# Two-layer linear attention and MLP on one core: dummies from a ready constant, some behind the first transposes, and the key weights in one load

## The chip, the core and the metric

The kernel runs on one core of one Trainium2 chip. The metric is the device time of one execution in microseconds (us), as the median of three runs; lower is better. All times inside an execution are counted from the start of the span that the profiler recorded. The engines are TensorE (PE, with its weight loads as PEld), VectorE (DVE), ScalarE (ACT), GpSimd (POOL) and SyncE (SP, which only issues DMAs here).

## The reference, cut to what matters

The input is one sequence of 2048 tokens with 512 features in bf16. Two blocks alternate, each twice, with the same weights:

```python
phi = lambda t: jnp.where(t > 0, t + 1, jnp.exp(t)) + 1e-6
# A: linear attention, 32 heads of 16
q, k, v = split(layernorm(x) @ wqkv)
pq, pk = phi(q), phi(k)
kv = einsum("bhsd,bhse->bhde", pk, v);  z = einsum("bhsd->bhd", pk)
o = einsum("bhqd,bhde->bhqe", pq, kv) / (einsum("bhqd,bhd->bhq", pq, z)[..., None] + 1e-6)
x = x + o @ wo
# B: MLP of width 1792
x = x + gelu(layernorm(x) @ w1 + b1) @ w2 + b2
```

The attention sums over all 2048 tokens, so nothing behind it can start before every key tile has been seen.

## The kernel before, in words

The tokens form 16 tiles of 128 rows, four tiles to a chunk. Layer 0 takes the chunks in the order `C0=(3, 0, 1, 2)`, so the first tiles are 12, 13, 14, 15, and then 0 to 11. Everything stays in SBUF.

`build_kernel` only describes the work as a graph of named operations, each with an engine, an estimated duration and what it reads and writes. A `Scheduler` (line 111) then takes the order of the operations on each engine from hand-stored lists, `CONF["ORDER"]` (line 325), one list for each of the five engines; its clock (a cost for each operation, and for DMAs a modelled bus, lines 178 to 183) serves to choose buffers and PSUM banks, and `assign_waits` (line 265) puts in the semaphore waits. On the chip each engine works through its list strictly in order, so an instruction that waits holds up all behind it on its engine. `CONF["WAY"]` says which engine does an operation that could go to several, and whether a transpose goes through PE (`pe`) or through a DMA (`dma`).

The names carry the layer and the tile. For tile 12 of layer 0:

- `x0`, `x1`, `x2` load tiles 12, 13, and 14 with 15 (lines 642 to 646); `xc0`, `xc1`, `xc2` load the other chunks (line 638); `wk0` and `wk1` are the two halves of the key weights, 256 KB each, on SP and on ACT (line 648); `wq` is the query weights, 512 KB (line 651). All but `wk1` are on SP.
- `statsA0_12`, `aggrA0_12`, `vepsA0_12`, `powA0_12` make the mean and 1/std (lines 720 to 735). In the first chunk the tile is only centred first (`cenA0_12`, line 701), the 1/std is applied later as the scale of the activations, and `yscA0_12` (lines 739 to 747) scales the centred tile itself for the G products. Tile 13 gets its sums from ACT instead (`sumA0_13`, `sqA0_13`, lines 708 and 715). Tiles 0 to 11 are normed at once by `normA0_...`, on DVE (line 760) or ACT (line 755).
- `PTA0_12` is four PE transposes of 128 by 128 (line 783) and `tcA0_12` the ACT copy out of PSUM (line 793); tiles transposed by DMA have `TA0_...` on SP instead (line 770).
- `K0_12` is the key product (four matmuls of 512 columns, line 838), `Q0_3_0` the query product of tile 12 (line 856, chunk 3; lines 869 for chunks that are not done by token). Each is followed by `exp...` and `relu...` on ACT (lines 808 and 819) and `min...`, `phi...` on DVE or POOL (lines 821 and 825, or 812 and 814).
- `G0_12_0` collects the product of keys and normed tokens (line 939). `Z0_c` sums a chunk's keys (line 920), `zs0_c` adds them up on DVE (line 929), `zb0` builds the block matrix for the denominators (line 1000), and `D0_...` are the denominators (line 1063) with `ln...` and `rec...` on ACT (lines 1065 and 1067). `KV0`, `M0` (lines 994 and 1017), `WO0` (line 1087) finish the attention; `PTB0_0`, `W10` (line 1119) and `W20` (line 1157) are the MLP. Layer 1 has the same names with 1.

In PSUM the key and query tiles of the first chunk, their transposes and the dummies share the four banks 4 to 7; banks 0 to 3 hold the running G.

PE begins with `warm` (line 678): seven dummy matmuls of 512 columns and one of 128 on `onesm`, a tile that DVE fills first (`ones`, line 641). Weights of the later stages (`wv`, `wo`, `w1_0`, `w1_1`, `w2_0`, `w2_1`, function `late`, line 664) are loaded from POOL's queue behind all transposes of layer 0. `b2` (line 1193) is the load of the last bias, copied to 128 partitions, and stands on SP between two transposes; `b1` and `Tb1` (lines 1191 and 1214) load and transpose the other bias and `b1c` on ACT (line 1215) copies it.

The lists before, up to where they matter for the change:

```python
"pe":  "warm PTA0_12 PTA0_13 K0_12 K0_13 PTA0_14 Q0_3_0 Q0_3_2 PTA0_15 K0_14 G0_12_0 Q0_3_1 K0_15 G0_13_0 "
       "G0_14_0 Q0_3_3 PTA0_1 K0_0 K0_1 G0_15_0 K0_3 ..."
"act": "wk1 sumA0_13 tcA0_12 tcA0_13 sqA0_13 reluk0_12 expk0_12 tcA0_14 expk0_13 reluk0_13 ..."
"sp":  "x0 x1 wk0 x2 wq xc0 xc1 xc2 TA0_0 TA0_3 TA0_2 TA0_8 TA0_4 b2 TA0_6 TA0_7 ..."
```

Of the kernel before, what the change touches and what calls it, by code (L numbers as in the profile page):

```python
# [6 lines left out]
BF16 = mybir.dt.bfloat16  # L7
# [3 lines left out]
P = 128  # L11
S = 2048
D = 512
# [97 lines left out]
class Scheduler:  # L111
# [12 lines left out]
    def run(self):  # L124
# [14 lines left out]
        for _ in g.ops:  # L139
# [38 lines left out]
            if e == "sp" or o.sem is not None:  # L178
                if o.name[0] == "T":
                    o.end = max(at + o.lat, bus + 1000.0 if bus > at + 300.0 else 0.0)  # L180
                else:
                    bus = max(at + (1300.0 if at < 1400.0 else 1700.0 if e == "pool" else 900.0), bus) + o.nbytes
                    o.end = bus + o.lat
            else:
                o.end = at + dur + o.lat
# [79 lines left out]
def assign_waits(graph, order, sems, dma_sems):  # L265
# [10 lines left out]
    while len(done) < total:  # L276
        moved = False
        for e in ENGINES:
# [43 lines left out]
    C0=(3, 0, 1, 2), N_WARM=7, ZC=(0, 3), LQ='sp', N_HALF=1, N_K=4, N_Q=3, P_Z0=6.15, N_PB=1, N_PT=8, P_DEN=-50.43,  # L322
# [4 lines left out]
            "warm PTA0_12 PTA0_13 K0_12 K0_13 PTA0_14 Q0_3_0 Q0_3_2 PTA0_15 K0_14 G0_12_0 Q0_3_1 K0_15 G0_13_0 "  # L327
            "G0_14_0 Q0_3_3 PTA0_1 K0_0 K0_1 G0_15_0 K0_3 G0_0_0 K0_2 Q0_0_2 Q0_0_0 G0_1_0 K0_8 Z0_3 K0_4 G0_2_0 "
            "K0_6 G0_3_0 Q0_0_3 K0_7 K0_5 G0_4_0 K0_10 K0_11 Z0_0 K0_9 Q0_1_2 Q0_1_3 Z0_1 Q0_0_1 Q0_1_0 Z0_2 "
            "G0_5_0 G0_6_0 D0_0_3 D0_0_0 G0_7_0 Q0_1_1 D0_0_1 G0_8_0 D0_0_2 G0_9_0 G0_10_0 G0_11_0 G0_11_2 G0_11_1 "  # L330
            "D0_1_0 Q0_2_0 G0_11_3 KV0_0 KV0_1 D0_1_1 ZR0 KV0_2 KV0_3 Q0_2_1 D0_1_2 M0_0 M0_1 M0_2 M0_3 Q0_2_2 "
            "WO0_0_0 WO0_0_1 WO0_0_2 WO0_0_3 D0_1_3 WO0_1_0 WO0_2_0 WO0_3_0 Q0_2_3 WO0_4_0 WO0_7_0 WO0_6_0 PTB0_0 "
            "WO0_5_0 W10_0_5_0 W10_0_1_0 W10_0_9_0 W10_0_6_0 W10_0_2_0 W10_0_3_0 W10_0_12_0 W10_0_7_0 W10_0_0_0 "
            "W10_0_4_0 W10_0_13_0 W10_0_11_0 W10_0_8_0 W10_0_10_0 W20_0_0 W20_1_0 W20_0_7 W20_1_7 W10_0_9_1 "
            "W10_0_1_1 W10_0_7_1 W10_0_8_1 W10_0_5_1 W10_0_6_1 W10_0_12_1 W10_0_0_1 W10_0_13_1 W10_0_3_1 "
            "W10_0_11_1 W10_1_4_0 W10_1_13_0 W10_0_4_1 W10_1_11_0 W10_1_0_0 W10_1_3_0 W10_1_2_0 W10_0_2_1 "
            "W10_1_6_0 WO0_9_0 WO0_8_0 WO0_11_0 W10_1_5_0 W10_1_8_0 W10_1_10_0 WO0_10_0 W10_0_10_1 W10_1_1_0 "
            "W10_1_12_0 W10_1_7_0 W10_1_9_0 W20_7_0 W20_4_0 W20_7_7 W20_4_7 WO0_15_0 W20_5_0 W20_2_0 W20_5_7 "
# [189 lines left out]
def build_kernel(nc, A_x, A_wqkv, A_wo, B_x, B_w1, B_b1, B_w2, B_b2, out, conf=None, report=False):  # L528
# [5 lines left out]
    with ExitStack() as es:  # L534
# [48 lines left out]
        def bank(t, n=512):  # L583
            return ps[:, t.slot, 0:n]
# [767 lines left out]
```

## Time and profile before

| what | value |
|---|---|
| median of three runs (lowest to highest) | 328.75 us (328.06 to 329.84) |
| the profiled execution, its own time | 330.35 us |
| its span, first to last instruction | 328.6 us |
| PE busy | 322.0 us of the span |
| first dummy, first key matmul | 1.51 us, 6.52 us |
| first W1 matmul of layer 0 | 65.61 us |
| end of the last matmul group | 326.0 us |

The span is 1.75 us shorter than the execution's own time, and the profiled execution is 1.6 us longer than the median. In a timeline row the first number is the start, the second how long the merged group lasted, then engine, line, operation, what is written from what, and in brackets how long the engine stood idle before and what released it. A matmul's recorded duration contains its drain (379 ns is common for one of 512 columns), so the rate of a stream is read from the starts of its groups, not from their durations. The row PEclk of the page shows the throttle's grant, and is at full speed in all 40 slices.

### The profile page before, as it was taken

How to read it: one execution, taken by the hardware profiler on the slowest of the kernel's cores; microseconds unless marked ns; L12 is line 12 of the kernel's file. 1: busy time of each engine (PE TensorE's matmuls, PEld its weight loads, DVE VectorE, ACT ScalarE, POOL GpSimd, SP SyncE). 2: the span in 40 equal slices, each digit the busy share in tenths (PEclk: the TensorE clock that was granted, in tenths of full speed). 3: DMA queues.
4: the chain of work that ended last, by engine and by line, in shares of the span. 5: the costliest groups of instructions: out<-in, count | busy, mean ns of one | idle time of the engine just before them, and what ended most of it. 6: DMA issues, size and time to landing. Idle time of an engine off the chain costs nothing.

```text
span 328.6 us, 4769 instructions
## 1 busy us (share of the span) xinstructions
PE 322.0 (98%) x1716; PEld 159.1 (48%) x1716; DVE 223.0 (68%) x507; ACT 194.4 (59%) x334; POOL 133.1 (41%) x223
## 2 busy tenths in 40 slices
PE   7999999999999999999999999999999999999996
PEld 2444545476544444444444444448644444444444
DVE  4799599999794554575158899999989776100132
ACT  4898769783747055536984377878933452567200
POOL 3366646567447105533047725756903176000000
PEclk9999999999999999999999999999999999999999
DMA  6324593105404300312101110022044214200011
GB/s 231 152 49 98 121 358 149 18 16 97 49 0 66 80 16 3 64 32 48 34 16 32 35 32 0 2 49 50 18 96 99 48 33 97 64 0 2 16 48 64
DMA packets 47027, 20.37 MB, mean 62 GB/s; under 512 B 41948, under 2 KB 45532, under 8 KB 47004
## 3 DMA queue, kind: packets, MB, share of 16 engines
q1 hardware_dynamic: 45676, 15.09, 20.7%
q0 software_dynamic: 1056, 4.72, 4.1%
q8 instruction: 13, 0.21, 0.3%
q10 hardware_dynamic: 272, 0.26, 0.3%
q14 instruction: 10, 0.08, 0.1%
HBM read 8.00 MB, written 2.10 MB: 31 GB/s over the span
## 4 chain that ended last, share of the span: by engine, by line
PE 94%; DMA 2%; DVE 1%; ACT 1%; issue 0%; SPq 0%; ACTq 0%
PE ps L1119 30%; PE ps L1157 29%; PE ps L838 9%; PE ps L1087 8%; PE ps L856 5%; PE ps L971 4%; PE ps L939 3%; PE ps L869 2%; DMA wqkv<-in_A_wqkv_dram 1%; DMA t<-yb 1%; PE ps L1144 1%; PE ps L1063 1%; PE ps L1017 1%; PE ps L994 1%; PE ps L783 0%
## 5 line engine op out<-in xcount | busy, mean ns | idle before, releaser
L1125 ACT ACTIVATE gT<-ps,b1c 128x512 bf16<-128x512 f32 (+1 forms) x140 | 77.0, 601 | 53.8 <-PE ps L1119 53.3
L1119 PE MATMUL ps<-t,w 128*128 128x512 bf16 (+1 forms) x560 | 101.3, 336 | 0.4 <-issue 0.4
L1157 PE MATMUL ps<-w,gT 128*128 128x512 bf16 x434 | 97.3, 379 | 0.0
L1119 PEld LDWEIGHTS ps<-t,w 128*128 128x128 bf16 x560 | 54.6, 98 | 43.6 <-ACT t L793 1.2
L1157 PEld LDWEIGHTS ps<-w,gT 128*128 128x128 bf16 x434 | 42.5, 98 | 50.8
L808 ACT ACTIVATE eb<-ps 128x512 bf16<-128x512 f32 x56 | 32.5, 602 | 31.0 <-PE ps L838 25.6
L735 POOL TENSOR_TENSOR rstd<-veps,neghalf 128x1 f32<-128x1 f32 x64 | 37.8, 598 | 8.3 <-DVE veps L733 5.9
L1167 DVE TENSOR_TENSOR outb<-ps,xsb 128x512 bf16<-128x512 f32 x15 | 10.2, 683 | 40.2 <-PE ps L1157 38.7
L838 PE MATMUL ps<-wqkv,t 128*128 128x512 bf16 x128 | 33.6, 394 | 1.4 <-DMA t<-yb 0.7
L720 DVE BATCH_NORM_STATS2 stats<-xsb 128x6 f32<-128x512 f32 x48 | 32.0, 680 | 0.3
L1087 PE MATMUL ps<-gtb,t 128*128 128x512 bf16 x128 | 30.9, 379 | 0.0
L760 DVE TENSOR_SCALAR yb<-xsb,mv,rstd 128x512 bf16<-128x512 f32 x28 | 16.7, 602 | 13.6 <-POOL rstd L735 13.4
L733 POOL TENSOR_SCALAR veps<-mv 128x1 f32<-128x1 f32 x28 | 7.4, 276 | 43.7 <-DVE mv L722 43.0
L755 ACT ACTIVATE yb<-xsb,nmr,rstd 128x512 bf16<-128x512 f32 x20 | 15.7, 811 | 14.6 <-POOL nmr L752 14.6
L819 ACT ACTIVATE rb<-ps 128x512 bf16<-128x512 f32 x38 | 21.8, 601 | 0.2 <-PE ps L838 0.2
L821 DVE TENSOR_SCALAR eb<-eb 128x512 bf16<-128x512 bf16 x46 | 14.4, 325 | 10.1 <-ACT eb L808 10.0
L725 POOL TENSOR_SCALAR veps<-mv 128x1 f32<-128x1 f32 x32 | 8.8, 274 | 29.1 <-DVE mv L722 27.2
L838 PEld LDWEIGHTS ps<-wqkv,t 128*128 128x128 bf16 x128 | 12.3, 100 | 17.0 <-issue 1.7
L856 PE MATMUL ps<-wqkv,t 128*128 128x512 bf16 x80 | 20.3, 383 | 0.0
L1163 DVE TENSOR_TENSOR xsb<-ps,xsb 128x512 f32<-128x512 f32 x16 | 11.0, 688 | 13.2 <-PE ps L1157 13.1
L1087 PEld LDWEIGHTS ps<-gtb,t 128*128 128x128 bf16 x128 | 12.3, 98 | 15.1 <-DVE mv L722 0.5
L1104 POOL TENSOR_TENSOR xsb<-xsb,b2b 128x512 f32<-128x512 f32 x14 | 17.4, 1255 | 2.8 <-ACT yb L755 1.6
(103 smaller groups left out, 395.2 us busy)
## 6 DMA issues: line engine op xcount, KB each, us to landing
w<-in_B_w_dram POOLq DMA_DIRECT2D x4, 896.0 KB, 9.8
out_dram<-outb SPq DMA_DIRECT2D x15, 128.0 KB, 2.0
t<-in_A_x_dram SPq DMA_DIRECT2D x3, 512.0 KB, 7.3
t<-yb SPq DMA_TRANSPOSE x56, 2.5
wqkv<-in_A_wqkv_dram SPq DMA_DIRECT2D x1, 512.0 KB, 5.8
wo<-in_A_wo_dram POOLq DMA_DIRECT2D x1, 512.0 KB, 4.6
wqkv<-in_A_wqkv_dram POOLq DMA_DIRECT2D x1, 512.0 KB, 7.4
t<-t SPq DMA_TRANSPOSE x20, 2.5
```

The costliest lines, as they stand in the source:

```text
L720: G.op("dve", lambda e: e.bn_stats(stats[:, s.slot, :], src()), 620, reads=src_keys, writes=[k + "s"], tiles=[s, *src_tiles], prio=prio, n ...
L735: G.op("pool", lambda e: e.tensor_tensor(rstd[:, s.slot:s.slot + 1], veps[:, s.slot:s.slot + 1], neghalf[:], op=ALU.pow), 570, reads=[k + ...
L760: G.op("dve", lambda e: e.tensor_scalar(yb[:, y.slot, :], src(), stats[:, s.slot, 2:3] if by_act else mv[:, s.slot, 0:1], rstd[:, s.slot:s ...
L808: G.op("act", lambda e: e.activation(eb[:, et.slot, :], bank(bt), ACT.Exp, scale=factor()), 478, reads=[src_key, *more], writes=[f"e{tag}" ...
L819: G.op("act", lambda e: e.activation(rb[:, rt.slot, :], bank(bt), ACT.Relu, scale=factor()), 478, reads=[src_key, *more], writes=[f"r{tag} ...
L838: ins = e.matmul(bank(b), lhsT=yTa(yT)[:, dt, k * P:(k + 1) * P], rhs=wqkv[:, dt, D:2 * D], start=(dt == 0), stop=(dt == DT - 1))
L856: ins = e.matmul(bank(b), lhsT=yTa(yT)[:, dt, k * P:(k + 1) * P], rhs=wqkv[:, dt, 0:D], start=(dt == 0), stop=(dt == DT - 1))
L1087: ins = e.matmul(bank(wb), lhsT=yTa(pq)[:, kt, k * P:(k + 1) * P], rhs=gtb[:, kt, :], start=(kt == 0), stop=(kt == DT - 1))
L1104: G.op("pool" if on_pool else "dve", lambda e: e.tensor_tensor(xsb[:, st, :], xsb[:, st, :], b2b[:], op=ALU.add), 1120 if on_pool else 600 ...
L1119: ins = e.matmul(bank(b, n), lhsT=w1[:, dt, ft * P:(ft + 1) * P], rhs=yTa(yT)[:, dt, k0 * P:k1 * P], start=(dt == 0), stop=(dt == DT - 1))
L1125: G.op("act", lambda e, ft=ft, b=b, k0=k0, k1=k1, n=n: e.activation(gT[:, g.slot, ft * 512 + k0 * P:ft * 512 + k1 * P], bank(b, n), ACT.Ge ...
L1157: ins = e.matmul(bank(b), lhsT=gT[:, g.slot, ft * 512 + k * P:ft * 512 + (k + 1) * P], rhs=w2[:, ft, :], start=(ft == 0), stop=(ft == FT - 1))
```

## The change

1. The dummies read the constant 1.0 that the program sets up before the engines start, spread to 128 by 512 by a stride of zero, in place of `onesm`. `warm` now has eight matmuls of 512 columns and one of 128, and waits for nothing. Two more groups follow: `idle0_0`, four matmuls of 128 columns behind `PTA0_12`, and `idle0_1`, three behind `PTA0_13`.
2. `wk0` is now all key weights in one load of 512 KB, second on SP, right behind `x0`. `x1` and `x2` move to ACT's queue, `x1` behind the DVE fill of `onesm` as `wk1` was.
3. `b2` moves behind all transposes of layer 0 on SP.
4. Tile 1 of layer 0 is transposed by DMA (`TA0_1` on SP), no longer by PE and ACT (`PTA0_1`, `tcA0_1`). `yscA0_14`, `vepsA0_14` and `pr0_3_2` move from DVE to POOL, `normB0_4` from DVE to ACT (with an `nmrB0_4` on POOL).
5. The planner's landing times of the first loads are fixed numbers (`LAND`), and all five lists are written anew to the end, with the same operations otherwise.

The diff, cut to its core:

```diff
-    C0=(3, 0, 1, 2), N_WARM=7, ...
+    N_WARM2=1, N_IDLE=[4, 3], XQ='act', WKQ='sp', WK1=1,
+    LAND={'x0': 3250, 'x1': 4200, 'wk0': 5800, 'x2': 5000, 'wq': 7200, 'xc0': 9700, 'xc1': 11000, 'xc2': 12200},
+    C0=(3, 0, 1, 2), N_WARM=8, ...
 "pe":
+            "warm PTA0_12 idle0_0 PTA0_13 idle0_1 K0_12 PTA0_14 K0_13 Q0_3_0 PTA0_15 K0_14 Q0_3_1 Q0_3_3 Q0_3_2 "
+            "K0_15 G0_12_0 G0_13_0 K0_0 G0_14_0 K0_1 G0_15_0 Z0_3 G0_0_0 K0_3 K0_2 G0_1_0 Q0_0_2 Q0_0_0 K0_8 K0_4 "
+            "G0_2_0 K0_6 G0_3_0 Q0_0_3 K0_7 K0_5 G0_4_0 K0_10 K0_11 Z0_0 K0_9 Q0_1_2 Z0_1 Q0_1_3 Z0_2 Q0_1_0 "
+            "Q0_0_1 G0_5_0 D0_0_3 G0_6_0 D0_0_0 G0_7_0 D0_0_1 G0_8_0 Q0_1_1 G0_9_0 D0_0_2 G0_10_0 ...
 "act":
+            "x1 x2 sumA0_13 tcA0_12 sqA0_13 tcA0_13 expk0_12 tcA0_14 reluk0_12 reluk0_13 expk0_13 reluq0_3_0 "
+            "tcA0_15 reluk0_14 expq0_3_0 reluq0_3_1 expk0_14 expq0_3_1 yscA0_15 expq0_3_2 expk0_15 reluk0_15 "
+            "normA0_3 expk0_0 ... expq0_1_3 ln0_0_3 rec0_0_3 b1c ln0_0_0 ...
 "dve":
+            "... yscA0_13 cenA0_15 yscA0_12 vepsA0_15 mink0_12 statsA0_0 statsA0_1 aggrA0_0 phik0_12 mink0_13 "
+            "statsA0_2 normA0_0 ... mink0_9 phik0_11 phik0_9 zs0_1 phiq0_0_0 zs0_2 zb0 ...
 "pool":
+            "... powA0_14 powA0_15 yscA0_14 vepsA0_0 powA0_0 ... phik0_6 w2_1 w1_1 wv w1_0 bdm1 wo w2_0 ...
 "sp":
+            "x0 wk0 wq xc0 xc1 xc2 TA0_0 b1 TA0_1 TA0_3 TA0_2 TA0_8 TA0_4 TA0_6 TA0_7 TA0_5 TA0_10 TA0_11 TA0_9 b2 "
+            "Tb1 ...
...
-            dma("sp", lambda e, k=k, n=n: e.dma_start(
+            dma(cf["XQ"], lambda e, k=k, n=n: e.dma_start(
...
+        wsp = cf["WKQ"].split()
+        n = DT // len(wsp)
+        for h, q in enumerate(wsp):
+            dma(q, lambda e, h=h, n=n: e.dma_start(wqkv[:, n * h:n * h + n, D:2 * D], wsrc[:, n * h:n * h + n, D:2 * D]), [f"wk_{h}"], prio=-99,
+                name=f"wk{h}", kb=128 * n, after=[ones] if q == "act" and cf["WK1"] else ())
...
-        def warm(e):
-            for n in [D] * cf["N_WARM"] + [P]:
-                ins = e.matmul(bank(wu, n), lhsT=onesm[:, 0:P], rhs=onesm[:, 0:n], start=True, stop=True)
+        def run_idle(e, sizes):
+            one = nc.const_aps.tensor(1.0, [P, D], BF16)
+            for n in sizes:
+                ins = e.matmul(bank(wu, n), lhsT=one[:, 0:P], rhs=one[:, 0:n], start=True, stop=True)
             return ins
-        G.op("pe", warm, cf["N_WARM"] * 427 + 107, reads=["onesm"], writes=["warm"], tiles=[wu], prio=-300, name="warm", n=cf["N_WARM"] + 1)
+
+        def idle(name, sizes, after=(), writes=()):
+            return G.op("pe", lambda e: run_idle(e, sizes), sum(sizes) / 1.2, writes=["warm", *writes], tiles=[wu], prio=-300, name=name,
+                        n=len(sizes), after=after)
+        idle("warm", [D] * cf["N_WARM"] + [P] * cf["N_WARM2"])
...
-                    tr = transpose_pe(y, ykey, yT, k, f"yT0_{st}", pr, f"A0_{st}", True)
+                    wait = [held] if held else ()
+                    tr = transpose_pe(y, ykey, yT, k, f"yT0_{st}", pr, f"A0_{st}", True, wait)
+                    held = idle(f"idle{n}_{k}", [P] * cf["N_IDLE"][k], [G.writer[f"yT0_{st}p"]]) if n == 0 and k < 2 else None
...
+        dma("sp", lambda e: e.dma_start(b2b[:], bass.AP(B_b2.tensor, B_b2.offset, [[0, P], [1, D]])),
+            ["b2b"], prio=-79, name="b2", kb=128, after=trs)
```

## The prediction, made before the run

> **What bounds the kernel now.** I read the page first, for who ends last.
>
> ```profile
> PE 322.0 (98%) x1716; PEld 159.1 (48%) x1716; DVE 223.0 (68%) x507; ACT 194.4 (59%) x334; POOL 133.1 (41%) x223
> ...
> PE 94%; DMA 2%; DVE 1%; ACT 1%; issue 0%; SPq 0%; ACTq 0%
> ```
>
> PE is busy for 98% of the span and makes 94% of the chain that ended last. So what counts is when PE starts, how fast its clock runs, and where it stands. The change acts before the first W1 matmul at 65.61; from there the stream runs to 326.0, and in the waits of PE's weight loads no wait after that start is longer than 0.8 us. Second, the timeline of PE alone, up to that matmul.
>
> ```profile
> 1.51 3.27 PE L680 MATMUL ps<-onesm 128*128 128x512 bf16 x8 [1.51 <-DVE onesm L641]
> 4.59 1.32 PE L783 MATMUL ps<-idp,yb 128*128 128x128 bf16 x8
> 6.52 3.57 PE L838 MATMUL ps<-wqkv,t 128*128 128x512 bf16 x8 [0.61 <-DMA wqkv<-in_A_wqkv_dram]
> 9.88 0.63 PE L783 MATMUL ps<-idp,yb 128*128 128x128 bf16 x4
> 10.31 2.18 PE L856 MATMUL ps<-wqkv,t 128*128 128x512 bf16 x8
> 12.33 0.39 PE L783 MATMUL ps<-idp,yb 128*128 128x128 bf16 x4
> 12.55 1.03 PE L838 MATMUL ps<-wqkv,t 128*128 128x512 bf16 x4
> 13.41 1.03 PE L939 MATMUL ps<-pkb,yb 128*128 128x512 bf16 x4
> ...
> 28.92 1.03 PE L939 MATMUL ps<-pkb,yb 128*128 128x512 bf16 x4
> 30.66 1.02 PE L838 MATMUL ps<-wqkv,t 128*128 128x512 bf16 x4 [0.71 <-DMA t<-yb]
> ...
> 43.08 1.89 PE L939 MATMUL ps<-pkb,yb 128*128 128x512 bf16 x8
> 45.59 0.61 PE L1063 MATMUL ps<-t,zb 128*128 128x512 bf16 x2 [0.62 <-DVE zb L1000]
> ```
>
> The first dummy waits for `onesm`, and `K0_12` at 6.52 for the key weights. Its eight matmuls (`K0_12`, `K0_13`) take 9.88 − 6.52 = 3.36 us, 0.42 us each; from 12.55 on four take 13.41 − 12.55 = 0.86 us, 0.216 each. So PE runs at half rate until about 9.9, which PEclk (9 in every slice) does not show: eight key matmuls lose 3.36 − 1.73 = 1.63 us. From starts and this rate I also read four places where PE stood: 12.04 to 12.33 (0.29), before `K0_1` at 19.87 (0.19), 29.79 to 30.66 (0.87, `K0_6` waits for its transpose), 44.81 to 45.59 (0.78, `D0_0_3` waits for `zb0`).
>
> Third, the other engines, since a faster PE only helps if they follow: ACT's timeline.
>
> ```profile
> 8.42 0.69 ACT L819 ACTIVATE rb<-ps,rstd 128x512 bf16<-128x512 f32 x1 [1.18 <-PE ps L838]
> 9.01 0.68 ACT L808 ACTIVATE eb<-ps,rstd 128x512 bf16<-128x512 f32 x1
> 10.56 0.60 ACT L793 ACTIVATE t<-ps 128x512 bf16<-128x512 bf16 x1 [0.87 <-PE ps L783]
> 11.05 0.68 ACT L808 ACTIVATE eb<-ps,rstd 128x512 bf16<-128x512 f32 x1
> ```
>
> From 10.56 on ACT starts an instruction about every 0.57 us with hardly any idling to 28.9 (in the table of stretches 5.00 of 5 us busy from 15 to 20). Two of them, 1.14 us, drain one key or query tile that PE makes in 0.86. So between 10 and 28 ACT is as much the bound as PE, and a gain must show on ACT's queue too.
>
> **The change, part by part,** against the execution's own 330.35 us.
>
> *Start of the keys.* The halves of `wk` were issued at 1.72 (SP) and 1.49 (ACT) and landed 4.7 us later, 6.43 the later. Now 512 KB are issued at about 1.25, the second place on SP. With the 4.7 us of the halves they land at 5.95; with the 5.8 us of `wq`, a load of the same size, at 7.05. The bytes to move until then (`x0`, `x1`, `x2`, `wk`) are the same 1024 KB. I take 6.2, nearer to the halves, which shared the engines with as many bytes: **−0.3** (−0.56 to +0.53). `tcA0_12` allows it: `x0` still goes first, so `PTA0_12` stays near 4.59, and the copy ended at 5.85.
>
> *Clock.* The dummies start at about 0.80, as SP's first issue does, 0.7 earlier: eight of 0.427 and one of 0.107 end at 4.32. `PTA0_12` follows at 4.58 (0.43 at half rate), `idle0_0` (4 × 0.107) to 5.44, `PTA0_13` to 5.87, `idle0_1` to 6.2. The dummies cost PE nothing, as it waits for `wk` there; if `wk` came at 5.95, up to 0.25 is uncovered. In the trace full rate came after 3.36 us of unbroken key matmuls, while 3.08 us of dummies and then holes (5.0 to 5.3, 5.73 to 6.52) did not bring it. Now one stretch from 0.80 holds a single hole of 0.26, so by 6.2 it has lasted 5.4 us. I take a few matmuls still slow: of 1.63 us I book **−1.35** (0 to −1.63).
>
> [...]
>
> *Off PE.* `PTA0_1` (18.59 to 18.82) goes: **−0.22**. ACT loses `tcA0_1`, 0.57. In return `TA0_1` is one more SP transpose (1.26 us median to issue) and 2.5 us to land; SP starts it after `normA0_1`, about 15.5, so it lands near 18.0, when PE reaches `K0_1` (below).
>
> *Stalls up to `K0_6`.* ACT: `sumA0_13` starts about 0.25 later (`x1` now issued 1.49, was 1.25), `sqA0_13` and `tcA0_13` end by 7.35, `exp` of tile 12 follows at once, and no wait for `PTA0_14` comes (its tile arrives with `x2`, issued at 1.95 rather than 2.19 and behind only `x1`). ACT was dense from 10.56 with two instructions done; now from about 7.5: a lead of 10.56 − 2 × 0.57 − 7.5 = 1.9, with `tcA0_1` 2.5 us. DVE: `statsA0_0` sat at 12.04, though its load landed at 3.17 + 6.6 = 9.8; now it stands there at 9.8 with about 0.7 us of older work (`phik0_12`, `mink0_13`) behind it: a lead of about 1.5 to 2. POOL gets `yscA0_14` (1.15 us like its other 128 × 512 operations) in a stretch where it idled 3.89 us. So all lead by about 2, but eight key and query tiles in a row (no G between) now share four banks that ACT drains at 1.14 us each: I walked the list and find PE standing about 1.2 us between 9 and 14 us. Against that, `b2` (issued 26.57) no longer delays `TA0_6`:
>
> ```profile
> 15.86 10.67 SPq L770 DMA_TRANSPOSE t<-yb  x5
> 26.57 0.58 SPq L1193 DMA_DIRECT2D b2b<-in_B_b_dram  x1
> 27.20 8.49 SPq L770 DMA_TRANSPOSE t<-yb  x6
> ```
>
> `normA0_6` ended at 25.76, `TA0_6` was issued at 27.20 and took 3.3 us to land, where 2.5 is the median. Now `normA0_6` ends near 25.1 and it lands near 27.7, before PE gets to `K0_6`. Old stalls 0.29 + 0.19 + 0.87 = 1.35, new 1.2: **−0.15** (−1.35 to +1.5).
>
> *Denominators.* `zb0` now stands right behind `zs0_2`, and between `Z0_2` and `D0_0_3` three groups (2.6 us) run in place of two (1.7). `Z0_2` itself comes two groups earlier and may wait for `phik0_9`, which ended 3.2 us after `K0_9`; PE gives it 2.1. Of 0.78 I book **−0.5** (−0.78 to +0.4).
>
> *The rest.* `wo` is now sixth of the late loads: 3.8 MB at the 351 to 379 GB/s of that stretch is some 11 us, from 35 on, so by 47; `M0` needs it at 55.3 less the gain. `w1` and `wv` have more room. `normB0_4` takes 0.8 us of ACT at about 70, where ACT was busy 3.0 of 5 us. The lists after 65 are permuted at equal work; the 3.9 us of weight-load waits on others after 65 mostly lie behind running matmuls, and I book **+0.15** (−0.4 to +1.5).
>
> Sum: −0.3 − 1.35 − 0.22 − 0.15 − 0.5 + 0.15 = −2.37. The profiled execution becomes 328.0; taken from the median of the runs, 328.75 − 2.37 = **326.4 us**.
>
> **Rivals.**
> 1. [...] Chance 0.17.
> 2. *ACT's draining decides*: the eight tiles cost PE 1 us more than I walked: gain 1.2, **327.5**. For it: ACT's rows from 10.56. Chance 0.15.
> 3. *More is gained*: the new stalls are mostly absent (−1.2): **325.2**. Chance 0.10.
> 4. *Slower, through `b1c`.* It ran at 52.4, 10 us after `Tb1` landed (37.46 + 4.6). Now it stands right behind `rec0_0_3`, which I expect to end near 44.3, and `Tb1` is issued at about 36 behind `b2`, which waits for all transposes, while 1.8 MB of `w2_1` and `w1_1` go ahead of it. With 4.6 us to land it comes at 40.6. The longest landing of the late loads was 12.0 us; from 12.4 us on (44.3 + 2.4 + 1.64 = 48.3) ACT's stand, and with it the denominators, eat the gain and 0.5% more. At 14 us the loss is 5.7 − 2.4: **332**. Chance 0.06.
>
> **How the numbers follow.** Forecast 0.52, rivals 0.17, 0.15, 0.10, 0.06. 0.5% is 1.64 us, about what a measurement of this kernel can tell from no change, so the bounds are 327.1 and 330.4. The forecast's own spread (start, clock, stalls) is about ±0.9, which leaves a tenth of it above 327.1; of rivals 1 and 2, a quarter falls below. Faster 0.47 + 0.10 + 0.08 = 0.65; slower 0.06 and a little for stalls in the permuted lists, 0.07; same 0.28. For 8 in 10 the range runs from below rival 3 to above rivals 1 and 2: 324.9 to 328.3.
>
> **What would show it.** First dummy near 0.8 and no wait on `onesm`. [...] The first `exp` near 7.5 and no ACT idle before `tcA0_14`. PE holes between 9 and 14 us of about 1.2; 2 or more, rival 2. `statsA0_0` at 9.8, `TA0_0` near 13.2. No 0.87 hole before `K0_6`, and less than 0.4 before `D0_0_3`. First W1 matmul near 63.1. An ACT idle ahead of L1215 would be rival 4. I am wrong if W1 starts at 63 and the end does not follow (the rewritten lists lose it), or if the keys land after 7.

## The result, and the profile after

The changed kernel is **slower**: 333.0 us (median of 6 runs, 332.7 to 333.8) against 329.3 us of the kernel before beside it, a ratio of 1.0107 (95% interval 1.0081 to 1.0134). The profiled execution took 332.78 us, with a span of 331.0. The forecast was 326.4, so the direction was wrong too.

The page of the changed kernel, busy time and the chain that ended last:

```profile
PE 322.7 (97%) x1720; PEld 158.3 (48%) x1720; DVE 220.4 (67%) x503; ACT 194.5 (59%) x334; POOL 135.6 (41%) x227
...
PE 83%; DVE 8%; DMA 3%; ACT 2%; POOL 2%; SPq 1%; issue 1%; DVEq 0%; POOLq 0%
```

PE is as busy as before, but its share of the chain fell from 94% to 83%, and DVE's rose from 1% to 8%: somewhere PE now waits for DVE. PE's timeline shows the first place, at the front:

```profile
0.83 3.68 PE L689 MATMUL ps<-const-bfloat16-1.0 128*128 128x512 bf16 x9 [0.83 <-PEq L1352]
4.64 0.40 PE L796 MATMUL ps<-idp,yb 128*128 128x128 bf16 x4
4.88 0.39 PE L689 MATMUL ps<-const-bfloat16-1.0 128*128 128x128 bf16 x4
7.74 0.51 PE L796 MATMUL ps<-idp,yb 128*128 128x128 bf16 x4 [2.47 <-DVE yb L714]
8.04 0.53 PE L689 MATMUL ps<-const-bfloat16-1.0 128*128 128x128 bf16 x3
8.36 1.91 PE L851 MATMUL ps<-wqkv,t 128*128 128x512 bf16 x4
10.21 0.61 PE L796 MATMUL ps<-idp,yb 128*128 128x128 bf16 x4
```

The dummies start at 0.83, and at 4.64 four transposes start 0.24 us ahead of the next group: PE has its full rate already. Then it stands 2.47 us for tile 13, and the keys that follow (8.36, not 6.52) run at half rate again. The granted clock of that stretch (the third number from the right; behind it the busy share of the DMA engines and GB/s) and the first operation of ACT say why:

```profile
4.00:6.00 2.00, 1.14 (x10) 0.45 (x8) 0.54 (x2) 0.00 (x0) 0.00 (x0) 1.00 0.94 287
6.00:8.00 2.00, 0.26 (x4) 0.26 (x5) 0.54 (x3) 1.62 (x4) 0.56 (x1) 0.97 1.09 411
8.00:10.00 2.00, 2.00 (x10) 0.82 (x7) 1.07 (x3) 0.88 (x3) 0.58 (x4) 0.50 1.03 414
```

```profile
6.38 0.63 ACT L721 ACTIVATE eb<-t 128x512 bf16<-128x512 bf16 x1 [4.31 <-DMA t<-in_A_x_dram]
```

The grant is 1.00, then 0.50 from 8 to 10 us. ACT, which makes the sums of tile 13, waited for `x1` until 6.38: issued at 1.49 on ACT's queue it took 4.9 us to land, where on SP, issued at 1.25, it had taken 2.7. In the kernel before the same operation started at 3.95:

```profile
3.95 0.63 ACT L708 ACTIVATE eb<-t 128x512 bf16<-128x512 bf16 x1 [1.88 <-DVE stats L720]
```

The second place lies far behind, in layer 1, where DVE adds the attention output to x (`RA1_...`, line 1105, or 1092 in the kernel before). First PE, then DVE and POOL of the changed kernel:

```profile
217.73 1.04 PE L1100 MATMUL ps<-gtb,t 128*128 128x512 bf16 x4 [0.58 <-DVE xsb L1105]
219.25 1.04 PE L1100 MATMUL ps<-gtb,t 128*128 128x512 bf16 x4 [0.48 <-DVE xsb L1105]
220.57 1.04 PE L1100 MATMUL ps<-gtb,t 128*128 128x512 bf16 x4 [0.28 <-DVE xsb L1105]
```

```profile
214.63 1.37 DVE L838 TENSOR_TENSOR t<-eb,rb 128x512 bf16<-128x512 bf16 x1
215.93 1.14 DVE L834 TENSOR_SCALAR eb<-eb 128x512 bf16<-128x512 bf16 x1
216.99 0.68 DVE L1105 TENSOR_TENSOR xsb<-ps,xsb 128x512 f32<-128x512 f32 x1
```

```profile
214.39 1.33 POOL L838 TENSOR_TENSOR t<-eb,rb 128x512 bf16<-128x512 bf16 x1 [1.30 <-ACT rb L832]
215.69 1.23 POOL L1064 TENSOR_TENSOR t<-t,rr 128x512 bf16<-128x512 bf16 x1
```

The same DVE operations (`phiq1_3_0`, `minq1_3_2`, which is one of two in its row, and `RA1_1`), POOL's (`phiq1_3_1`) and PE's in the kernel before:

```profile
213.32 0.36 DVE L825 TENSOR_TENSOR t<-eb,rb 128x512 bf16<-128x512 bf16 x1
...
214.20 0.49 DVE L821 TENSOR_SCALAR eb<-eb 128x512 bf16<-128x512 bf16 x2
214.60 1.28 DVE L1092 TENSOR_TENSOR xsb<-ps,xsb 128x512 f32<-128x512 f32 x2
```

```profile
214.56 1.15 POOL L825 TENSOR_TENSOR t<-eb,rb 128x512 bf16<-128x512 bf16 x1 [2.38 <-DVE eb L821]
```

```profile
217.08 2.10 PE L1087 MATMUL ps<-gtb,t 128*128 128x512 bf16 x8
```

Beside POOL's operations, 0.36 became 1.37 and some 0.25 became 1.14; `RA1_1`, queued behind them, came 2.4 us later than before (216.99 for 214.60), and PE waited for it and the next two, where it had not waited before.

### The profile page after: what moved, and what is told of

It reads as the page before. It is cut to its first block, busy times and chain, and to the rows that moved or that the text cites. A ratio compares the mean times of both kernels' runs of the same rounds, so it can differ in the third digit from the quotient of the medians.

```text
span 331.0 us, 4774 instructions
## 1 busy us (share of the span) xinstructions
PE 322.7 (97%) x1720; PEld 158.3 (48%) x1720; DVE 220.4 (67%) x503; ACT 194.5 (59%) x334; POOL 135.6 (41%) x227
## 4 chain that ended last, share of the span: by engine, by line
PE 83%; DVE 8%; DMA 3%; ACT 2%; POOL 2%; SPq 1%; issue 1%; DVEq 0%; POOLq 0%
PE ps L1132 28%; PE ps L1170 26%; PE ps L851 7%; PE ps L1100 7%; PE ps L952 4%; PE ps L984 3%; PE ps L882 3%; PE ps L869 2%; DMA t<-in_A_x_dram 2%; DVE stats L733 1%; PE ps L1157 1%; DVE eb L834 1%; DMA t<-t 1%; DVE xsb L1105 1%; DVE gtb L997 1%
## 5 line engine op out<-in xcount | busy, mean ns | idle before, releaser
L748 POOL TENSOR_TENSOR rstd<-veps,neghalf 128x1 f32<-128x1 f32 x64 | 36.6, 580 | 7.7 <-DVE veps L746 5.4
L851 PE MATMUL ps<-wqkv,t 128*128 128x512 bf16 x128 | 33.1, 390 | 0.1
L768 ACT ACTIVATE yb<-xsb,nmr,rstd 128x512 bf16<-128x512 f32 x21 | 16.5, 812 | 13.9 <-POOL nmr L765 13.9
L834 DVE TENSOR_SCALAR eb<-eb 128x512 bf16<-128x512 bf16 x46 | 15.5, 347 | 10.7 <-ACT eb L821 10.3
L869 PE MATMUL ps<-wqkv,t 128*128 128x512 bf16 x80 | 20.1, 379 | 0.0
L773 DVE TENSOR_SCALAR yb<-xsb,mv,rstd 128x512 bf16<-128x512 f32 x27 | 15.9, 597 | 3.0 <-POOL rstd L748 2.5
L1117 POOL TENSOR_TENSOR xsb<-xsb,b2b 128x512 f32<-128x512 f32 x14 | 16.6, 1192 | 2.4 <-ACT yb L768 1.3
```

What stands on the lines that cost most here:

```text
L748: G.op("pool", lambda e: e.tensor_tensor(rstd[:, s.slot:s.slot + 1], veps[:, s.slot:s.slot + 1], neghalf[:], op=ALU.pow), 570, reads=[k + ...
L834: G.op("dve", lambda e: e.tensor_scalar(eb[:, et.slot, :], eb[:, et.slot, :], 1.0, 1e-6, op0=ALU.min, op1=ALU.add), 210, reads=[f"e{tag}"] ...
L851: ins = e.matmul(bank(b), lhsT=yTa(yT)[:, dt, k * P:(k + 1) * P], rhs=wqkv[:, dt, D:2 * D], start=(dt == 0), stop=(dt == DT - 1))
L869: ins = e.matmul(bank(b), lhsT=yTa(yT)[:, dt, k * P:(k + 1) * P], rhs=wqkv[:, dt, 0:D], start=(dt == 0), stop=(dt == DT - 1))
L1117: G.op("pool" if on_pool else "dve", lambda e: e.tensor_tensor(xsb[:, st, :], xsb[:, st, :], b2b[:], op=ALU.add), 1120 if on_pool else 600 ...
```

## The experiments

One table for all. "W1" is the start of the first W1 matmul of layer 0 in the profiled execution, "rest" the time from there to the start of the last matmul. The ratio is to the kernel before, run beside it; as that kernel's own median lay between 328.6 and 330.0 from one session to the next, small differences are better read from the ratios. Holes are counted from the starts and the full rate (0.86 us for four matmuls of 512 columns), so they come out some 0.16 us longer than the idle time in a row's brackets (at full rate a matmul of 512 columns is recorded with 0.38 us, and the next starts 0.216 behind it).

| kernel | us (lowest to highest) | ratio (95% interval) | W1 | rest |
|---|---|---|---|---|
| before | 329.3 (328.1 to 330.2) | 1 | 65.61 | 260.1 |
| changed | 333.0 (332.7 to 333.8) | 1.0107 (1.0081 to 1.0134) | 65.29 | 262.9 |
| new_front_old_tail | 332.9 (332.4 to 335.0) | 1.0099 (1.0060 to 1.0137) | 66.08 | 262.4 |
| old_front_new_tail | 333.7 (332.2 to 336.1) | 1.0104 (1.0048 to 1.0161) | 63.76 | 263.8 |
| new_with_old_loads | 331.0 (330.4 to 332.4) | 1.0056 (1.0025 to 1.0088) | 62.95 | 263.3 |
| new_old_loads_b | 331.1 (329.9 to 332.6) | 1.0051 (1.0019 to 1.0083) | 63.23 | 263.4 |
| old_new_loads | 331.1 (330.8 to 331.9) | 1.0086 (1.0069 to 1.0103) | 66.11 | 260.1 |
| after_x1_sp | 331.8 (330.8 to 333.8) | 1.0096 (1.0063 to 1.0128) | 66.17 | 263.0 |
| after_long_idle | 332.4 (332.3 to 334.5) | 1.0122 (1.0086 to 1.0157) | 65.00 | 262.7 |
| before_again | 328.4 (327.7 to 330.6) | 0.9992 (0.9961 to 1.0024) | 64.61 | 260.2 |
| old_with_dummies | 329.6 (329.0 to 331.5) | 0.9995 (0.9965 to 1.0025) | 62.88 | 261.7 |
| dummies_cover | 328.3 (328.2 to 329.6) | 0.9996 (0.9977 to 1.0014) | 62.85 | 260.5 |
| dummies_split | 332.1 (331.6 to 332.7) | 1.0113 (1.0094 to 1.0133) | 64.37 | 263.6 |
| cover_b2 | 328.2 (328.1 to 328.7) | 0.9977 (0.9960 to 0.9994) | 62.86 | 260.7 |
| new_ra1_first | 330.6 (329.1 to 331.2) | 1.0061 (1.0036 to 1.0086) | 63.73 | 261.9 |
| new_minq_late | 328.8 (328.0 to 329.6) | 0.9982 (0.9960 to 1.0004) | 63.49 | 261.2 |
| new_old_layer1 | 329.3 (328.5 to 329.8) | 0.9992 (0.9968 to 1.0016) | 62.52 | 261.3 |
| after_minq_late | 331.1 (330.6 to 331.9) | 1.0048 (1.0029 to 1.0068) | 65.03 | 261.0 |
| new_minq_cover | 328.0 (327.7 to 329.1) | 0.9951 (0.9927 to 0.9976) | 63.86 | 260.3 |

### Front or lists

The theory after the two traces: the lists behind W1 lose it all (A). The rival: the late front does (B). Two hybrids cut all five lists at the first W2 product of layer 0 (about 72 us).

new_front_old_tail: the changed kernel with the old order from there on; PE's list as an example:

```diff
-  ... W20_0_0 W20_1_0 W20_0_7 W20_1_7 W10_0_1_1 W10_0_7_1 ...
+  ... W20_0_0 W20_1_0 W20_0_7 W20_1_7 W10_0_9_1 W10_0_1_1 ...
```

> The changed kernel with its own lists up to the first W2 matmul of layer 0 and the lists of before behind it (normB0_4 and pr0_3_2 back on DVE). Theory A, the loss sits in the rewritten lists behind W1: PE no longer stands before the attention output of layer 1 (217 to 221 us, 1.8 us lost there), and as the first W1 matmul came 0.3 us earlier than before, the time is 328.5 to 329.3, ratio 0.998 to 1.000. Rival B, the front hands a late state to the rest (buffers, weights): it stays at 332 to 333, ratio 1.009 to 1.012.

The time is B's, but not by B's mechanism. The three waits for RA1 were gone, a hole of 1.82 us at 85.53 took their place (of the kind that "The hole at 82" treats), and the rest was still 262.4.

```profile
85.53 6.65 PE L1281 MATMUL ps<-t,w 128*128 128x512 bf16 x34 [1.66 <-ACT gT L1287]
```

old_front_new_tail: the kernel before with the new order from there on, the same diff the other way round.

> The kernel before with its own lists up to the first W2 matmul of layer 0 and the changed lists behind it (normB0_4 on ACT and pr0_3_2 on POOL as there). Theory A: the loss comes along, first W1 matmul at 65.6 as before and about 2.6 us more behind it, 331.5 to 332.3, ratio 1.007 to 1.010. Rival B: 329.3, ratio 1.000.

The three waits came along with the new lists (0.74, 0.64, 0.66 us at 217 to 220), with the old front. So the lists lose about 2 us there by themselves.

```profile
82.62 2.54 PE L1268 MATMUL ps<-t,w 128*128 128x512 bf16 x11 [1.30 <-ACT gT L1274]
...
217.15 1.04 PE L1236 MATMUL ps<-gtb,t 128*128 128x512 bf16 x4 [0.58 <-DVE xsb L1241]
```

The time lies above both forecasts and is as long as that of the whole change. With the three waits, a hole of 1.46 us at 82.62 makes up most of the 3.7 us by which the rest is longer than before. What the front loses, these two runs don't tell.

### The loads

new_with_old_loads, in the changed kernel:

```diff
-    XQ='act', WKQ='sp',
+    XQ='sp', WKQ='sp act',
-    "sp": "x0 wk0 wq ...   "act": "x1 x2 ...
+    "sp": "x0 x1 wk0 x2 wq ...   "act": "wk1 ...
```

> The changed kernel with x1, x2 and the key weights loaded as before (x1, half of wk and x2 on SP, the other half on ACT), all else kept. Theory A: x1 is there at about 3.9 in place of 6.3, so the second transpose no longer waits 2.5 us, the first key matmul comes at about 6.5 in place of 8.4 and at full rate (the hole in which the clock fell back is gone); first W1 matmul at 63.3 to 64.3 in place of 65.3, time 331 to 332, ratio 1.005 to 1.008, since the loss behind W1 stays. Rival C, ACT and DVE bound the front whatever PE does: W1 stays within 0.3 us of 65.3 and the time at 332.5 to 333.3.

The time fell by 2.0 us and W1 by 2.3; the keys started at 6.35 at full rate. What remained against before lay behind W1.

old_new_loads: the reverse, in the kernel before and nothing else.

```diff
-  "sp": "x0 x1 wk0 x2 wq ...   "act": "wk1 ...
+  "sp": "x0 wk0 wq ...   "act": "x1 x2 ...
```

> The kernel before with only the loads of the change: the small tile x1 and x2 on ScalarE's queue, the key weights in one load behind x0 on SP; dummies and lists as before. Theory A (the move of the loads costs about 2 us by itself, as between the changed kernel and the one with the old loads, 333.0 against 331.0): x1 lands at 6.2 to 6.5 and not at 4, the first key matmul starts at 8.2 to 8.5 and not at 6.5, and the time is 330.8 to 331.6. Theory B (it costs only because it throws away the clock that the early dummies had won; the kernel before has a slow clock there anyway): the keys come late but the time rises by less than 0.8, at most 330.1.

Theory A by the time: ratio 1.0086. The waits, in its PE timeline:

```profile
7.12 0.40 PE L829 MATMUL ps<-idp,yb 128*128 128x128 bf16 x4 [2.05 <-DVE yb L747]
7.36 3.11 PE L884 MATMUL ps<-wqkv,t 128*128 128x512 bf16 x8
10.26 0.63 PE L829 MATMUL ps<-idp,yb 128*128 128x128 bf16 x4
```

Tile 13 came 1.8 us after its place (5.3 in the kernel before). The keys started at 7.36, not at 8.2 or later as expected: `x1` landed at 5.8 here. But theory B's premise, that there is no early clock to lose, did not hold in this execution: PE had its full rate at 7.12 (the four transposes start 0.24 us ahead of the keys) and lost it, so that the eight keys took 2.90 us and not 1.73. The granted clock from 8 to 10 us:

```profile
8.00:10.00 2.00, 2.00 (x6) 0.71 (x5) 1.61 (x4) 2.00 (x5) 0.74 (x2) 0.50 1.03 416
```

So a late tile and a lost clock are both in these 2.5 us, and the run does not part them.

after_x1_sp: in the changed kernel, `x1` alone back on SP, ahead of the one load of the key weights.

```diff
-  "sp": "x0 wk0 wq ...   "act": "x1 x2 ...
+  "sp": "x0 x1 wk0 wq ...   "act": "x2 ...
```

> The changed kernel with the small tile x1 back on SP, right behind x0 and ahead of the key weights, which stay in one load; x2 stays on ScalarE. Theory M (what costs is that x1 lands late, at 6.4, on ScalarE's queue and beside the 512 KB of key weights): x1 lands at about 4, tile 13 is transposed by 6.0, the keys start when their weights land, at 6.3 to 7, at full rate, and the time falls by 1.5 to 2.2, to 330.8 to 331.5. Theory N (the one load of the key weights is what costs): the keys start at 7.5 or later whatever x1 does, and the time falls by less than 0.8.

Between the two: 331.8 is 1.2 us less than the changed kernel, but by the ratio to the kernel before (1.0096 for 1.0107, with intervals that overlap) it is only 0.1%. How much comes back with `x1` alone is not settled. The profiled execution was its slowest (333.77), and there the one load of 512 KB landed late:

```profile
5.83 0.40 PE L843 MATMUL ps<-idp,yb 128*128 128x128 bf16 x4 [0.34 <-DVE yb L761]
...
7.63 1.86 PE L898 MATMUL ps<-wqkv,t 128*128 128x512 bf16 x4 [1.24 <-DMA wqkv<-in_A_wqkv_dram]
```

Tile 13 is in time (5.83), the weights are not (7.63), and the keys ran at half rate after that hole too. How the 2.0 us of the loads divide between `x1`, one load for two halves and `x2` stays open.

after_long_idle: `idle0_0` of the changed kernel as 12 matmuls of 512 columns, to hold the clock through the hole.

```diff
-    [P] * cf["N_IDLE"][k]
+    [[D] * 12, [P] * 3][k]
```

> The changed kernel with twelve dummies of 512 columns behind PTA0_12 in place of four of 128, so that they last from 4.88 to about 7.4 and fill the hole in which PE waits for tile 13. Theory K (the granted clock falls because of that hole of 2.5 us): the grant stays at 1.00 up to 12, the first key group of four takes about 1.04 us and not 1.91, the first W1 matmul comes 1.2 to 1.8 us earlier than the 65.29 of the changed kernel, and the time is 331.2 to 331.9 against 333.0. Theory L (the grant falls for another reason, or ScalarE's draining takes what a faster PE gains): the first W1 matmul stays at 65.0 or later and the time at 332.6 to 333.3.

```profile
5.75 2.79 PE L689 MATMUL ps<-const-bfloat16-1.0 128*128 128x512 bf16 x12
8.38 0.38 PE L796 MATMUL ps<-idp,yb 128*128 128x128 bf16 x4
8.60 0.34 PE L689 MATMUL ps<-const-bfloat16-1.0 128*128 128x128 bf16 x3
8.77 1.02 PE L851 MATMUL ps<-wqkv,t 128*128 128x512 bf16 x4
```

The mechanism of theory K is shown in this execution: with the hole filled, the grant stays at 1.00 from 4 to 14 us and the keys run at full rate (four start 0.86 us ahead of the next group, not 1.85). Its size is not: tile 12 was there 0.9 us later in this execution (its transposes started at 5.52), and from the first key matmul to W1 only 0.7 us were gained (56.2 for 56.9). The time of 332.4 lies between both forecasts, and by its ratio (1.0122 for 1.0107) nothing was gained. How the cost of the loads divides between the late tile and the lost clock stays open: old_new_loads, beside the next run with the same lists, started its keys only 0.35 us later (7.36 and 7.01) and its W1 1.5 us later (66.11 and 64.61), which speaks for a larger share of the clock.

before_again: the kernel before, unchanged.

> The kernel before, once more, for a second profile of it. If its executions differ only at the front (when the first loads land and when PE gets its full rate), then an execution near the median has its keys at full rate earlier than 9.9, its first W1 matmul at 62.9 to 64.3 and not at 65.61, and from there to the last matmul the same 260.2 to 260.6 us. If they differ behind the front, the first W1 matmul is near 65.6 again and the stretch behind it is shorter than 259.5.

```profile
4.58 0.63 PE L783 MATMUL ps<-idp,yb 128*128 128x128 bf16 x4
5.95 0.40 PE L783 MATMUL ps<-idp,yb 128*128 128x128 bf16 x4 [0.74 <-DVE yb L701]
7.01 1.89 PE L838 MATMUL ps<-wqkv,t 128*128 128x512 bf16 x8 [0.66 <-ACT t L793]
```

Here PE has its full rate at 5.95 at the latest (four transposes recorded with 0.40 us, as at full rate, and not 0.63 as at 4.58), and eight key matmuls need 1.89 us, where the execution I had predicted from took 3.36. W1 came 1.0 us earlier, the rest is the same (260.2), and the time minus W1 is the same too: 330.35 − 65.61 = 264.7 and 329.38 − 64.61 = 264.8. By that, an execution of 328.75, the median shown, has its W1 at 64.0. That W1 is worked out, not seen.

old_with_dummies: the kernel before with the constant, eight dummies and both idle groups.

```diff
-  warm PTA0_12 PTA0_13 K0_12 ...
+  warm PTA0_12 idle0_0 PTA0_13 idle0_1 K0_12 ...
```

> The kernel before with only the dummies changed: from the constant, eight and one at once, four behind the first transposes and three behind the second; all lists and loads else as before. Theory A: one stretch without a hole over 0.3 us runs to the first key matmul at 6.5, so that is at full rate, the two key tiles take 1.7 us and not 3.4, and up to 1.2 us of it reaches W1 (64.4): 327.8 to 328.6, ratio 0.995 to 0.998. Rival C, the gain is taken back by ACT and DVE, whose queues were dense from 10.6 us on: the keys are at full rate, but W1 is at 65.3 to 65.6 and the time 329.0 to 329.6.

The dummies do what they should, W1 at 62.88, but the time is that of before (0.9995). Part of the gain went into a new hole at 81.62.

### The hole at 82

```profile
81.62 3.62 PE L1162 MATMUL ps<-t,w 128*128 128x512 bf16 x18 [1.58 <-ACT gT L1168]
```

The row names ACT, which was idle itself. The DMA transposes of that stretch (70 to 84 us) took, to landing:

```profile
DMA to landing us min/median/max: 2.4/2.5/4.6
```

The longest is that of `TB0_6` (tile 6 for the MLP, the last of the second chunk, issued at 76.7), which W1 needs next. dummies_cover puts 1.3 us of other matmuls over it:

```diff
-  W10_0_11_1 W10_1_4_0 W10_1_13_0 W10_0_4_1 ...
+  W10_0_11_1 W10_0_4_1 W10_0_2_1 W10_0_10_1 W10_1_4_0 W10_1_13_0 ...
```

> The kernel before with the new dummies, and on PE three groups of the first MLP chunk (W10_0_4_1, W10_0_2_1, W10_0_10_1, with their GELUs on ScalarE) ahead of the second chunk's first group. Theory C (the hole of 1.74 us at 81.62 is the wait for the last of the second chunk's transposes, which landed after 4.6 us; the page's blame on ScalarE is wrong): some 1.3 us of matmuls now lie over that wait, the hole shrinks to 0.5 or less, and the time falls from 329.57 to 328.0 to 328.7. Theory D (ScalarE's GELUs set it, as the page says): the hole stays at 1.5 or more, wherever it lies, and the time stays at 329.3 to 329.9.

```profile
75.81 10.56 PE L1236 MATMUL ps<-t,w 128*128 128x256 bf16 x71
```

No hole: theory C. The time is 328.3, as expected, and its spread is small; against the kernel before beside it (328.6) that is no difference.

Why was it late? In the trace of old_with_dummies, a DMA packet of kind "instruction" (16 KB; 13 of them in the execution, on queue 8) came at 77.8; the transpose issued at 78.03 took 2.23 us to issue on SP and not 1.2, and `TB0_6` was in flight. dummies_split gives PE 15 more instructions ahead.

```diff
-  idle("warm", [D] * 8 + [P])
+  idle("warm", [176] * 24)
```

> The kernel before with the new dummies, whose first 9 matmuls (8 of 512 columns, 1 of 128) are cut into 24 of 176 columns: the same columns, 15 instructions more on PE, nothing else changed. Theory E (the transposes that land late are those in flight while PE's next 16 KB of instructions are fetched): the fetch that came at 78 moves to about 75 to 77, ahead of the last transpose's issue, the last of the six transposes lands after 2.5 to 3.2 us and not after 4.6, the hole at 81.6 is under 0.7, and the time falls to 328.0 to 328.9. Theory F (the late landing has another cause, such as the other queues' loads at that time): the transpose takes 4 to 5 us again, the hole stays, 329.3 to 329.9.

With the 15 instructions more on PE the packet came 12.4 us behind W1 and not 14.9, so I take it for PE's instructions, and it hit the transpose before (`TB0_7`, 2.08 us to issue). But `TB0_6` stands behind that on the same queue, was issued at 79.02, and the hole was still 1.28 us: theory E is borne out in where the packet goes, and wrong in its time. Two holes were new:

```profile
228.52 7.15 PE L1162 MATMUL ps<-t,w 128*128 128x256 bf16 x64 [0.94 <-ACT gT L1168]
...
248.01 2.33 PE L1162 MATMUL ps<-t,w 128*128 128x512 bf16 x10 [0.90 <-DMA t<-yb]
```

The second follows a transpose that took 2.65 us to issue at 241.46, with a packet at 242.1; the first I can't explain. `x0` also landed 0.5 us later, and the keys started 0.76 us later than in old_with_dummies.

### One operation in VectorE's list

All on the changed kernel with the old loads, unless said. new_ra1_first:

```diff
-  pr1_1_1 phiq1_3_0 minq1_3_2 RA1_1 statsB1_1 aggrB1_1 RA1_0 ...
+  pr1_1_1 RA1_1 RA1_0 phiq1_3_0 minq1_3_2 statsB1_1 aggrB1_1 ...
```

> The changed kernel with the loads of before, and in VectorE's list RA1_1 and RA1_0 ahead of phiq1_3_0 and minq1_3_2. Theory G (the three holes of 0.74, 0.64 and 0.66 us at 215.8 to 218.7 come from the two bf16 operations, which GpSimd's operation beside them stretches from 0.36 and 0.25 to 1.37 and 1.14, with RA1 queued behind them): RA1_1 starts about 2.3 us earlier, the holes are under 0.5 in sum, and the time falls from 331.0 to 329.0 to 329.8. Theory H (VectorE has more to do there in the new order than PE allows, whatever comes first): the holes move to other operations and the time stays at 330.6 to 331.4.

The two operations took 0.42 and 0.29 us, and the rest fell by 1.4 us, not 2; DVE now waited for PE (0.31 and 0.60 us) in RA1. So the operations do as theory G says, but the time of 330.6 is H's. This execution's W1 came 0.8 us later than that of new_with_old_loads, because its first keys ran at half rate in spite of the dummies, as the starts show:

```profile
6.77 1.91 PE L948 MATMUL ps<-wqkv,t 128*128 128x512 bf16 x4
8.48 0.63 PE L893 MATMUL ps<-idp,yb 128*128 128x128 bf16 x4
```

new_old_loads_b is the kernel to compare the next two with.

> The changed kernel with the loads of before, once more, as the one to compare the next two with on the same chip: 330.5 to 331.4, with the holes of 0.74, 0.64 and 0.66 us at about 216 to 219, and 263 to 263.7 us from the first W1 matmul to the last.

As expected. new_minq_late moves one operation (past five others, not the eight of the expectation):

```diff
-  minq1_3_1 red1_1_3 rec1_1_2 den1_1_3 pr1_1_1 phiq1_3_0 minq1_3_2 RA1_1
+  red1_1_3 rec1_1_2 den1_1_3 pr1_1_1 phiq1_3_0 minq1_3_1 minq1_3_2 RA1_1
```

> The changed kernel with the loads of before, and in VectorE's list one operation moved: minq1_3_1 stands right ahead of minq1_3_2, as in the kernel before, and not eight places earlier. GpSimd's phiq1_3_1 waits for it. Theory G (GpSimd starts too early, and its operation beside VectorE's two bf16 operations stretches them): phiq1_3_1 starts at about the end of these two, they take 0.36 and 0.25 us again, the three holes are under 0.4 us in sum, and the time is 1.5 to 2.2 below that of new_old_loads_b. Theory H (the new order gives VectorE too much there): the operations are short again but RA1 still comes late, and the time falls by less than 0.7.

331.1 fell to 328.8, 2.3 us, by one operation. Its DVE and POOL:

```profile
212.41 0.41 DVE L935 TENSOR_TENSOR t<-eb,rb 128x512 bf16<-128x512 bf16 x1
212.74 0.48 DVE L931 TENSOR_SCALAR eb<-eb 128x512 bf16<-128x512 bf16 x2
```

```profile
213.10 1.15 POOL L935 TENSOR_TENSOR t<-eb,rb 128x512 bf16<-128x512 bf16 x1 [1.60 <-DVE eb L931]
```

POOL now waits for DVE (`<-DVE eb`, not `<-ACT rb`) and starts at 213.10, when the row of short operations is all but over (213.22); PE has no wait for RA1 left. This is what theory G forecast.

new_old_layer1 takes all five lists in the old order from layer 1's KV products (`KV1_0`) on.

> The changed kernel with the loads of before, and all five lists from about the KV products of layer 1 on (206 us) in the order of the kernel before. If the one operation is all that the rewritten lists cost: the time of new_minq_late within 0.5. If the rest of the new order costs too: at least 0.8 less than new_minq_late.

The rest is 261.3 against 261.2, the time 329.3 against 328.8, so 0.5 more and not less: the one operation was all that the new order cost there.

after_minq_late does the same in the changed kernel, loads and all.

> The changed kernel itself, loads and all, with one operation moved on VectorE: minq1_3_1 right ahead of minq1_3_2. If the two causes (the loads, and this operation) add up, the time is 330.6 to 331.3 against the 333.0 of the changed kernel: 2.0 to 2.3 less, as it was with the old loads. If the late front changes how GpSimd and VectorE meet, the gain is under 1.2 and the time over 331.8.

333.0 fell to 331.05, by 1.95 us: the two causes add up. PE in the place of the three waits:

```profile
216.68 2.75 PE L1149 MATMUL ps<-gtb,t 128*128 128x512 bf16 x12
```

### What is left of the change

cover_b2: dummies_cover with `b2` behind all transposes.

```diff
-  TA0_4 b2 TA0_6 TA0_7 TA0_5 TA0_10 TA0_11 TA0_9 b1 ...
+  TA0_4 TA0_6 TA0_7 TA0_5 TA0_10 TA0_11 TA0_9 b2 b1 ...
```

> The kernel before with the new dummies, the three groups of the first MLP chunk ahead of the second chunk, and b2 behind all transposes as the change has it: what the other runs left standing of the change, and no more. If the holes of the trace add up: without the hole of 0.85 us before K0_6 the time is 327.3 to 327.9, against 328.34 for the same kernel with b2 in its old place and 328.6 to 329.6 for the kernel before. If ScalarE or the denominators take the time back (as b2 only moves the wait), it is 328.1 to 328.6.

The time is 328.2, the second forecast: the hole before `K0_6` went, but one of 0.48 came at 31.95, for the next transposes, and the denominators' grew from 0.66 to 0.74. Against the kernel before it is 0.2% faster.

new_minq_cover: new_minq_late with two groups ahead of the second chunk.

```diff
-  W10_0_4_1 W10_0_3_1 W10_1_6_0 ... W10_0_2_1 ... W10_0_10_1 ...
+  W10_0_4_1 W10_0_3_1 W10_0_2_1 W10_0_10_1 W10_1_6_0 ...
```

> The changed kernel with the loads of before, minq1_3_1 moved back, and two more groups of the first MLP chunk on PE (W10_0_2_1, W10_0_10_1, with their GELUs on ScalarE) ahead of the second chunk's first group. If the hole of 0.53 us at 81.47 goes and nothing else comes: 327.8 to 328.5, below the 328.76 of the kernel without that, and below the kernel before by a little. If the hole is ScalarE's, it stays and the time is 328.5 to 329.1.

The hole at 81.47 went, and the rest is 260.3, near the 260.1 of the kernel before. At 328.0 it is 0.5% faster than the kernel before beside it (0.9951; that ran at 330.0 there and at 328.4 to 329.6 elsewhere, so 0.5% may be much), and the fastest of all: the change without its loads, and with two places in the lists mended.

## Why the prediction was wrong

- **Start of the keys** (−0.3). The weights landed at 6.55, inside my bounds. But the keys waited for tile 13. The step that failed is "`sumA0_13` starts about 0.25 later (`x1` now issued 1.49, was 1.25)": I moved the issue and kept the landing time of the old place. It came 2.4 us later (6.38 for 3.95): issued 0.24 us behind the 512 KB of key weights, and on ACT's queue, `x1` needs 4.9 us and not 2.7. Whether the order or the queue does it, no run parts; ahead of the weights on SP (after_x1_sp) it needed about 3.0. I had counted the bytes up to the weights' landing and not asked what the others lose. Measured for the move of all the loads: 2.0 us of time, the lost clock included.
- **Clock** (−1.35). Right in its mechanism, but not as sure as booked: full rate at 4.64, and with the old loads W1 at 62.85 to 62.88 in old_with_dummies, dummies_cover and cover_b2. Of 15 profiled executions with the early dummies 13 had full rate before the first key; in new_ra1_first and new_front_old_tail four keys took 1.71 us, half rate. The size was wrong twice. In the changed kernel the full rate was gone again behind the hole of 2.47 us (four keys in 1.85 us from 8.36). And the 1.63 us stood in an execution 1.6 us above the median; I subtracted them from the median, whose executions have mostly lost less (W1 at about 64.0, so some 1.1 us to win). Of four executions with the old dummies, three were at or near full rate when their keys started (before_again, old_front_new_tail, old_new_loads). I also misread the end of the half rate: in the execution I predicted from, the first query matmul still took 0.43 us (10.31 to 10.74), so half rate lasted to about 10.9 and not 9.9, and the 0.29 us "where PE stood" before 12.33 were slow matmuls, no stall, so that the old stalls' 1.35 holds 0.29 too much. The same kernel differs from run to run here: full rate came at about 10.9 us in this execution of the kernel before, and at 5.95 at the latest in another (before_again). Nor did one length of hole go with the loss: it was 2.47 us in the changed kernel, and in after_x1_sp no hole was longer than 1.24.
- **Off PE, stalls, denominators** (−0.22, −0.15, −0.5). From the first key matmul to W1 it was 56.85 us with the old lists (old_with_dummies) and 56.60 with the new (new_with_old_loads): −0.25 for the booked −0.87. The holes before `K0_6` and `D0_0_3` went; 0.61 us of waiting for `phik0_9` ahead of `Z0_2` came, which I had named and booked too small. With the old loads PE also waited for tile 14 ahead of `PTA0_14` (idle 0.79 us in new_with_old_loads), where I expected no wait. ACT's draining (rival 2) cost little: between 9 and 39 us two holes of 0.26 and 0.28 were left (new_old_loads_b).
- **The rest** (+0.15, up to +1.5). This is the second failure. "The lists after 65 are permuted at equal work" was true, and it cost 2.7 us in the trace, 1.8 of them in the three waits, and 2.0 to 2.3 in the time. I had not compared who stands beside whom.
- **Rivals.** `b1c` never waited (it ran at 46.9). No run shows a cause that would keep the clock slow until about 9.9, on which rival 1, its 0.17 and its place in the range rested; the runs showed no full rate before the first key in 2 of 15 executions (new_ra1_first and new_front_old_tail), and in the changed kernel a rate that was won and lost again. Of the two ways to be wrong that I named, the lists came as named, and the late start came through `x1`, not the keys.

The sum: 333.0, less 2.0 for the loads, less 2.3 for one operation (2.0 with the new loads), is 328.7 to 329.0, where the kernel before stands.

## What to carry to other kernels

When a load is moved, ask for its landing time in the new place, among all bytes that are ahead of it or beside it, not for its issue. When lists are rewritten "at equal work", look at which DVE and POOL operations now meet: one operation moved by five places cost as much as the move of the loads (2.0 to 2.3 us, and 2.0). And take a gain from several executions before subtracting it from a median: a profile that is above the median holds some of the gain in itself.

## What the runs showed of the hardware

- **Two DVE operations took longer beside POOL's.** In the changed kernel POOL's operation started 0.24 us ahead of DVE's (214.39 and 214.63). `phiq1_3_0` ended at 216.00, 0.28 after POOL's operation (215.72); `minq1_3_2` at 217.07, 0.15 after POOL's next (216.92). Beside POOL's they last 1.37 and 1.14 us, and their usual lengths are 0.36 and 0.25, so they look as if each had waited and then run at about its usual length. `RA1`, with one operand in PSUM, took its usual 0.64 us beside the same POOL operation in the kernel before. In new_minq_late, where POOL's operation starts only behind `phiq1_3_0` (213.10), that takes 0.41 us. What makes the two longer no run shows.
- **Instruction packets and late DMA transposes go together.** In the 19 profiled executions 78 transposes took over 1.45 us to issue (usual: 1.2), and 77 of them stood within 0.8 us of one of the 13 or 14 packets of 16 KB. Of 89 transposes that such a packet met in flight, 54 landed after 3.5 to 5.7 us, and 35 in the usual 2.4 to 2.6. That more instructions on PE move the packet, and the delay with it, rests on dummies_split alone (15 more, the packet 2.5 us earlier behind W1, and `TB0_7` the one that issued slowly). My estimate from it: a few instructions more or less on PE can move a delay of some 2 us (in old_with_dummies `TB0_6` landed after 4.6 us, not 2.5) onto another transpose, and PE pays if that tile is next, as with the hole at 81.62.
